# Chunked attention and a gated feed-forward in one kernel: transposes and value products on TensorE in 64x64 tiles instead of whole-array matmuls and transposing transfers

## Chip, cores and metric

One core of a Trainium2 chip. The metric is the device time of one execution in microseconds (us). Engines: TensorE (PE in the profile, its weight loads PEld), VectorE (DVE), ScalarE (ACT), GpSimd (POOL), SyncE (SP). Each executes its own instructions in the order in which they were recorded.

## What is computed

Four batches of 768 tokens, 8 heads of 64. Attention goes by chunks of 32 tokens: a chunk sees 8 memory rows, 16 tokens to the left, itself, and 8 tokens to the right, 64 keys in all.

```
for c in range(S // 32):
    k_full = concat(mem_k, k[c*32-16 : c*32+40])          # cut at the ends of the sequence
    a = softmax((q[c*32 : c*32+32] @ k_full.T) / 8)
    out[c*32 : c*32+32] = a @ concat(mem_v, v[c*32-16 : c*32+40])
x = out as [3072 tokens, 512]                              # heads side by side
result = (relu(x @ w_gate) * (x @ w_val)) @ w_out          # 512 -> 1536 -> 512
```

## The kernel before, in words

**Tiles and blocks.** The 3072 tokens are 24 tiles of 128 (six per batch, four chunks each). Tiles are gathered into blocks, `BLOCKS = [2, 2, 4, 4, 4, 4, 4]`, on which the feed-forward (FFN) works: `first` (L396) makes 12 x 2 groups of four matmuls (gate and value, 256 or 512 tokens wide), ScalarE's `relu` (L402) and VectorE's `gate` (L408) join them, `second` (L421) multiplies with w_out, `store` copies and sends the rows out on SP's queue.

**Attention of one tile.** q and k must stand with the head dimension on the partitions, so they are transposed. In batch 0 `pair_t` (L225) does it in 64-column tiles from pairs of tokens; for tiles 6 to 11 `qk_t` (L264) does it in whole-array transposes; from tile 12 on (`LATE_QK`) `qk_transfer` (L272) does it by a transposing transfer on SP's queue, and keys are copied from there to their place in `kT`. Then: `scores` (L298, 32 matmuls in 64x32 tiles of the array, two PSUM banks), `row_max`, `subtract` (VectorE), `exponent` (L326, three ScalarE instructions, which also bring the keys into the order of `v_bd`), `row_sum`, `reciprocal`, `normalise` (VectorE), the transpose of P (`p_t`, L347, whole-array; from tile 18 on `p_transfer`, L351, on SP's queue), `values`, and `x_copy` into the block's `xT`.

**Values.** For batches 1 to 3 two heads share a 128-row block of `v_bd`, `[128, 4, 24, 128]`, with zeros where a head's rows meet the other head's columns; L377 multiplies it in 16 whole-array matmuls of 32 columns. There are two such buffers: POOL zeroes each (L129, four memsets), POOL's queue loads the value rows over the zeros (L173), and eight transfers per batch (L156) put the memory rows in, from `vmem`. In batch 0 v comes as it lies, is brought to its chunks by `shift` (L204, products with a band matrix), and L363 and L370 multiply memory and value rows.

**PSUM.** Three pools: `fps`, four banks, FFN and shifts; `sps`, two banks, scores; `aps`, two banks, transposes and value products.

**What sets the order.** A planner in the kernel (`schedule`) walks through assumed durations, landing times and free buffers, takes for each engine the ready operation with the least priority value (attention ahead of FFN), and records the instructions in that order. So the order is fixed when the kernel is built, and at run time an engine waits for its next instruction whatever stands behind it. Loads are a list of their own on POOL's queue, with at most eight in flight. A transposing transfer is assumed to land 6 us after its issue (`LAND`); attention of a tile is held back until the FFN has come to a given group (`pace`).

Of the kernel before, what the change touches and what calls it, by code (L numbers as in the profile page):

```python
# [19 lines left out]
def kernel(  # L20
# [20 lines left out]
    CH = 32  # L41
# [7 lines left out]
    CTX = 16 + CH + 8  # L49
    NSET = 2  # L50
    BLOCKS = [2, 2, 4, 4, 4, 4, 4]
    GROUPS = [(0, 2), (2, 6), (6, 9), (9, 12)]
    BAND0 = 48

    LATE_QK, LATE_P = 12, 18

    KEY_RUNS = ((0, CH, 0), (KW, 64, CH), (CH, KW, CTX))
# [3 lines left out]
    ldpool = ctx.enter_context(tc.tile_pool(name="ldpool", bufs=18))  # L61
# [4 lines left out]
    ktpool = ctx.enter_context(tc.tile_pool(name="ktpool", bufs=3))  # L66
    grpool = ctx.enter_context(tc.tile_pool(name="grpool", bufs=3))
    opool = ctx.enter_context(tc.tile_pool(name="opool", bufs=3))

    fps = ctx.enter_context(tc.tile_pool(name="fps", bufs=4, space=bass.MemoryType.PSUM))  # L70
    sps = ctx.enter_context(tc.tile_pool(name="sps", bufs=1, space=bass.MemoryType.PSUM))
    aps = ctx.enter_context(tc.tile_pool(name="aps", bufs=2, space=bass.MemoryType.PSUM))
# [3 lines left out]
    def copy(eng, o, i):  # L76
# [5 lines left out]

    band = const.tile([128, BAND0 + 176], F16, name="band")
    ident_h = band[:, BAND0:BAND0 + 128]
    ident_b = const.tile([128, 128], BF16, name="ident_b")
    ident_f = const.tile([128, 128], F32, name="ident_f")
    w_gate_sb = const.tile([128, NFC, DFF], F16, name="w_gate_sb")
# [4 lines left out]
    vmem = const.tile([128, B, H, D], F16, name="vmem")  # L92
    vmem_0 = const.tile([128, HP, 2 * D], F16, name="vmem_0")
    v_bd = [const.tile([128, HP, NCH, 2 * D], F16, name=f"v_bd_{s}") for s in range(NSET)]
    vmem_f = v_bd[1][:, HP - 1].rearrange("p c d -> p (c d)").bitcast(F32)[:, 0:HP * 2 * D].rearrange(
        "p (h d) -> p h d", h=HP)
    v_q = v_bd[0][:, 0:2].rearrange("p h c d -> p (h c d)").rearrange("p (h c d) -> p h c d", h=HP, d=D)
    v_n = {}
    qk_p = {(i, r): const.tile([128, H, 2 * D], BF16, name=f"qk_p_{i}_{r}") for i in range(2) for r in range(TPB // 2)}
# [4 lines left out]
    def load_gate_val(i, which, par):  # L104

        m0, m1 = GROUPS[i]
        n = 128 * (m1 - m0)
        src, dst = ((moe_w_gate, w_gate_sb), (moe_w_val, w_val_sb))[which]
        nc.gpsimd.dma_start(
            dst[D * par:D * par + D, :, 128 * m0:128 * m1],  # L110
            bass.AP(tensor=src.tensor, offset=src[HP * D * par, 128 * m0].offset,
                    ap=[[DFF, D], [D * DFF, NFC], [1, n]]),
        )

    def make_band():
        nc.gpsimd.memset(band, 0.0)
        nc.gpsimd.affine_select(
            out=band, in_=band, compare_op=ALU.not_equal, fill=1.0, base=BAND0,
            pattern=[[-1, BAND0 + 176]], channel_multiplier=1)

    def load_out(i):
        n = NDC // 2
        nc.gpsimd.dma_start(
            w_out_sb[:, n * i:n * i + n, :],
            moe_w_out.rearrange("(c p) f -> p c f", p=128)[:, n * i:n * i + n, :],
        )

    def zero(eng, t, hp):
        eng.memset(t[:, hp].rearrange("p c d -> p (c d)").bitcast(F32), 0.0)  # L129


    def mem_load():
        for par in range(2):
            nc.sync.dma_start(
                kmem_f[:, par, :],
                bass.AP(tensor=mem_k.tensor, offset=mem_k[0, par, 0, 0].offset,
                        ap=[[2 * NMEM * D, B * HP], [D, NMEM], [1, D]]),
            )

    def mem_keys_t():  # L140
        TMP["kmem"] = aps.tile([128, B * HP * NMEM], F32, tag="aps", name="kmem_ps")
        nc.tensor.transpose(TMP["kmem"], kmem_f.rearrange("p a d -> p (a d)"), ident_f)

    def mem_values(par):
        p = 64 * par + CTX
        nc.gpsimd.dma_start(
            vmem[p:p + NMEM].rearrange("p b h d -> p (b h) d"),
            bass.AP(tensor=mem_v.tensor, offset=mem_v[0, 0, 0, 0].offset,
                    ap=[[D, NMEM], [NMEM * D, B * H], [1, D]]),
        )  # L150

    def mem_rows(eng, b, n):
        hp, par = divmod(n, 2)
        p = slice(64 * par + CTX, 64 * par + CTX + NMEM)
        src = vmem[p, b, HP * par + hp]
        eng.dma_start(  # L156
            v_bd[b % NSET][p, hp, :, D * par:D * par + D],
            bass.AP(tensor=src.tensor, offset=src.offset,
                    ap=[src.ap[0], [0, NCH], [1, D]]))


    def pattern_load():
        for par in range(2):
            p = 64 * par + CTX
            nc.sync.dma_start(
                vmem_f[p:p + NMEM, :, D * par:D * par + D],
                bass.AP(tensor=mem_v.tensor, offset=mem_v[0, HP * par, 0, 0].offset,
                        ap=[[D, NMEM], [NMEM * D, HP], [1, D]]))

    def load_v_rows(b, par, s0, s1, c0, c1):  # L170

        dst = v_bd[b % NSET].rearrange("p h c d -> p (h c) d")
        nc.gpsimd.dma_start(  # L173
            dst[64 * par + s0:64 * par + s1, c0:c1, D * par:D * par + D],
            bass.AP(tensor=v.tensor, offset=v[b, HP * par, 0, 0].offset + (CH * c0 + s0 - 16) * D,
                    ap=[[D, s1 - s0], [CH * D, c1 - c0], [1, D]]))

    def v_parts(b, par, c0, c1):
        parts = []
        if (b, par, c1) == (B - 1, 1, HP * NCH):  # L180
            c1 -= 1
            parts.append((b, par, 0, 48, c1, c1 + 1))
        return parts + [(b, par, 0, CTX, c0, c1)]


    def load_v_tile(t):
        v_n[t] = ldpool.tile([128, H, D], F16, tag="qk_b", name="v_n")
        nc.gpsimd.dma_start(
            v_n[t],
# [3 lines left out]
    def shift(c0):  # L193
        ps = TMP["sh", c0] = fps.tile([128, 2, HP, D], F32, tag="fps", name="vs_ps")
        for i in range(2):
            t, g = divmod(c0 + i, 4)
            parts = [(t, BAND0 + CH * g - 16)]
            if g == 0 and t:
                parts.append((t - 1, BAND0 + 112))
            if g == 3 and t < TPB - 1:  # L200
                parts.append((t + 1, BAND0 - 48))
            for n, (src, x) in enumerate(parts):
                for par in range(2):
                    nc.tensor.matmul(ps[D * par:D * par + D, i], lhsT=band[:, x:x + 64],  # L204
                                     rhs=v_n[src][:, HP * par:HP * par + HP, :],
                                     start=(n == 0), stop=(n == len(parts) - 1))

    def shift_copy(c0, eng):
        copy(eng, v_q[:, :, c0:c0 + 2, :].rearrange("p h c d -> p c h d"), TMP.pop(("sh", c0)))


    qk_b, qT, kT = {}, {}, {}

    def load_pair(r, i):
        x = (q, k)[i]
        nc.gpsimd.dma_start(
            qk_p[i, r],
            bass.AP(tensor=x.tensor, offset=x[0, 0, 256 * r, 0].offset,
                    ap=[[2 * D, 128], [S * D, H], [1, 2 * D]]))

    def pair_t(r, i, j):
        ps = TMP["pair", r, i, j] = aps.tile([128, HP, 128], BF16, tag="aps", name="qk_ps")
        for h in range(H):
            p = D * (h % 2)
            nc.tensor.transpose(ps[p:p + D, h // 2, :], qk_p[i, r][:, h, D * j:D * j + D], ident_b)  # L225

    def pair_copy(r, i, j, eng):
        ps = TMP.pop(("pair", r, i, j))
        if i == 0:
            o = qT[0][:, :, 256 * r + j:256 * r + 256]  # L230
            copy(eng, bass.AP(tensor=o.tensor, offset=o.offset, ap=[o.ap[0], [S, HP], [2, 128]]), ps)
        else:
            o = kT[0][:, :, 8 * r:8 * r + 8, j:KW]
            copy(eng,
                 bass.AP(tensor=o.tensor, offset=o.offset,
                         ap=[o.ap[0], [NCH * KW, HP], [KW, 8], [16 + NMEM, 2], [2, 8]]),
                 ps.rearrange("p h (c x s) -> p h c x s", c=8, x=2))

    def load_qk(a, i):
        b, t = divmod(a, TPB)  # L240
        x = (q, k)[i]
        qk_b[a, i] = ldpool.tile([128, H, D], BF16, tag="qk_b", name="qk_b")
        nc.gpsimd.dma_start(  # L243
            qk_b[a, i],
            bass.AP(tensor=x.tensor, offset=x[b, 0, 128 * t, 0].offset,
                    ap=[[D, 128], [S * D, H], [1, D]]))
# [11 lines left out]
    P_n, PT, S_ps, SM, TMP = {}, {}, {}, {}, {}  # L258

    def qk_t(a, i):  # L260
        ps = TMP["qk", a, i] = aps.tile([128, HP, 128], BF16, tag="aps", name="qk_ps")
        x = qk_b.pop((a, i))
        for hp in range(HP):
            nc.tensor.transpose(ps[:, hp, :], x[:, 2 * hp:2 * hp + 2, :].rearrange("p h d -> p (h d)"), ident_b)  # L264

    def qk_transfer(a, i):
        b, t = divmod(a, TPB)
        if i == 0:
            o = qT[b][:, :, 128 * t:128 * t + 128]
        else:  # L270
            o = TMP["qk", a, i] = ktpool.tile([128, HP, 128], BF16, name="k_t")
        nc.sync.dma_start(o, qk_b.pop((a, i)).rearrange("p h d -> p (h d)"), transpose=True)  # L272

    def qk_copy(a, i, eng):
# [505 lines left out]
```

## Time and profile before

| | |
|---|---|
| median of 3 runs | 252.5 us (252.33 to 255.31) |
| profiled execution, its own time | 254.24 us |
| its span, first to last instruction | 252.5 us |
| mean granted TensorE clock | 0.986 |
| busy: PE, DVE, ACT, POOL | 234.0, 131.3, 115.0, 90.7 us |
| software queue (POOL's): packets, MB | 94368, 16.42 |
| hardware queue (SP's): packets, MB | 21888, 10.51 |

The page's slices are a fortieth of the span each, 6.3 us. A group's row has its line, engine, operation, tiles, shape and count, then busy us and the mean ns of one. A timeline row has start and length in us, and in brackets the idle time of the engine before it and what ended it. The length of a matmul row holds the time in which its results drain while the next one runs already, so what a matmul costs its successor is read from start to start.

### The profile page before, as it was taken

The page shows a single profiled execution, that of the slowest core. Times are in us where ns is not written, and L with a number is a line of the kernel's source. Part 1 is how long each engine was busy: PE and PEld are TensorE (multiplying, and loading weights), DVE is VectorE, ACT ScalarE, POOL GpSimd, SP SyncE. Part 2 cuts the span into 40 slices and gives each one's busy share as a digit, 9 for nine tenths or more (in the row PEclk, how much of TensorE's full clock was granted, in tenths as well). Part 3 has the DMA queues.
Part 4 walks back from the last instruction along what each step waited for, and adds up shares of the span by engine and source line. Part 5 has one row for each costly group of instructions (what it writes and reads, how often), then busy time and mean ns, then how long its engine had stood idle before and what let it go on. Part 6 is the DMA issues. An engine that isn't in the chain of part 4 may idle for free.

```text
span 252.5 us, 6081 instructions
## 1 busy us (share of the span) xinstructions
PE 234.0 (93%) x2529; PEld 128.7 (51%) x2529; DVE 131.3 (52%) x245; ACT 115.0 (46%) x250; POOL 90.7 (36%) x105
## 2 busy tenths in 40 slices
PE   1869999999899999799999949999999999999994
PEld 0647887884445555345444424455444544444443
DVE  2462657985158886588543817964049340133400
ACT  2856757763236555356334444543153531333212
POOL 8975899605179950298450060000000000000000
PEclk9999999999999999999999976999999999999999
DMA  7999999999999999999999999222221101300022
GB/s 79 174 179 203 201 84 130 204 156 97 176 203 139 140 135 86 123 211 136 123 116 123 122 138 169 42 44 41 86 83 23 21 0 54 116 1 0 0 85 84
DMA packets 116285, 27.32 MB, mean 108 GB/s; under 512 B 107297, under 2 KB 113185, under 8 KB 116257
## 3 DMA queue, kind: packets, MB, share of 16 engines
q0 software_dynamic: 94368, 16.42, 113.4%
q1 hardware_dynamic: 21888, 10.51, 24.3%
q8 instruction: 20, 0.33, 0.6%
q14 instruction: 9, 0.07, 0.1%
HBM read 32.06 MB, written 6.29 MB: 152 GB/s over the span
## 4 chain that ended last, share of the span: by engine, by line
PE 79%; DMA 12%; DVE 4%; ACT 3%; issue 1%; POOL 0%; SPq 0%; ACTq 0%; POOLq 0%
PE v_ps L396 25%; PE g_ps L396 25%; PE out_ps L421 18%; DMA k_t<-qk_b 9%; PE s_ps L298 2%; PE xT_ps L377 2%; DMA qk_p<-in_q_dram 2%; PE xT_ps L370 2%; PE vs_ps L204 1%; PE qk_ps L225 1%; PE pT_ps L347 1%; DVE mx L311 1%; DVE dif L318 1%; PE qk_ps L264 1%; PE xT_ps L363 1%
## 5 line engine op out<-in xcount | busy, mean ns | idle before, releaser
L408 DVE TENSOR_TENSOR gvT<-v_ps,g_relu 128x512 f16<-128x512 f32 (+1 forms) x84 | 51.3, 611 | 51.9 <-PE v_ps L396 48.9
L396 PE MATMUL g_ps<-xT,w_gate_sb 128*128 128x512 f16 (+1 forms) x336 | 77.4, 353 | 0.8 <-ACT xT L78 0.8
L396 PE MATMUL v_ps<-xT,w_val_sb 128*128 128x512 f16 (+1 forms) x336 | 77.8, 355 | 0.0
L402 ACT ACTIVATE g_relu<-g_ps 128x512 f16<-128x512 f32 (+1 forms) x84 | 45.0, 535 | 56.2 <-PE g_ps L396 55.9
L421 PE MATMUL out_ps<-w_out_sb,gvT 128*128 128x512 f16 (+2 forms) x300 | 64.9, 371 | 0.0
L396 PEld LDWEIGHTS <-w_gate_sb 128*128 128x128 f16 x336 | 31.7, 99 | 28.3 <-issue 2.0
L396 PEld LDWEIGHTS <-w_val_sb 128*128 128x128 f16 x336 | 31.7, 99 | 27.2 <-issue 1.5
L421 PEld LDWEIGHTS <-gvT 128*128 128x128 f16 x300 | 28.2, 98 | 31.3
L78 ACT COPY o_sb<-out_ps 128x512 f32<-128x512 f32 (+2 forms) x25 | 14.1, 565 | 36.4 <-PE out_ps L421 32.5
L311 DVE TENSOR_REDUCE mx<-s_ps 128x8 f32<-128x512 f32 x24 | 16.4, 683 | 18.7 <-PE s_ps L298 18.2
L326 ACT ACTIVATE p_exp<-dif 128x256 f16<-128x256 f32 (+2 forms) x72 | 19.6, 336 | 10.7 <-DVE dif L318 10.5
L243 POOL DMA_DIRECT2D qk_b<-in_k_dram x18 | 16.4, 911 | 14.4 <-issue 8.0
L330 DVE TENSOR_REDUCE sm<-p_exp 128x8 f32<-128x512 f16 x24 | 16.3, 681 | 9.2 <-ACT p_exp L326 9.0
L156 POOL DMA_DIRECT2D v_bd<-vmem x16 | 10.1, 637 | 28.6 <-DMA v_bd<-in_v_dram 27.4
L243 POOL DMA_DIRECT2D qk_b<-in_q_dram x18 | 16.4, 909 | 3.8 <-issue 2.5
L341 DVE TENSOR_TENSOR p_n<-p_exp,rinv 128x512 f16<-128x512 f16 x24 | 16.5, 687 | 0.4
L318 DVE TENSOR_TENSOR dif<-s_ps,mx 128x512 f32<-128x512 f32 x24 | 16.5, 686 | 0.4
L173 POOL DMA_DIRECT2D v_bd<-in_v_dram x7 | 13.9, 1996 | 5.2 <-issue 3.7
L298 PE MATMUL s_ps<-kT,qT 64*32 64x64 bf16 (+2 forms) x768 | 8.6, 199 | 5.7 <-ACT kT L78 3.3
L298 PEld LDWEIGHTS <-qT 64*32 64x32 bf16 x768 | 5.3, 92 | 14.0 <-issue 11.8
L78 ACT CAST xT<-xT_ps 128x512 f16<-128x512 f32 x14 | 8.2, 586 | 8.5 <-PE xT_ps L377 4.5
L377 PEld LDWEIGHTS <-v_bd 128*128 128x128 f16 x288 | 9.4, 97 | 3.6 <-issue 0.3
(52 smaller groups left out, 159.8 us busy)
## 6 DMA issues: line engine op xcount, KB each, us to landing
out_dram<-o_sb SPq DMA_DIRECT2D x23, 256.0 KB
v_bd<-in_v_dram POOLq DMA_DIRECT2D x5, 672.0 KB, 18.0
qk_b<-in_k_dram POOLq DMA_DIRECT2D x18, 128.0 KB, 7.5
qk_b<-in_q_dram POOLq DMA_DIRECT2D x18, 128.0 KB, 7.8
w_out_sb<-in_moe_w_out_dram POOLq DMA_DIRECT2D x2, 768.0 KB, 11.6
qk_p<-in_k_dram POOLq DMA_DIRECT2D x3, 256.0 KB, 6.1
qk_p<-in_q_dram POOLq DMA_DIRECT2D x3, 256.0 KB, 6.5
v_n<-in_v_dram POOLq DMA_DIRECT2D x6, 128.0 KB, 6.5
```

The source lines that it names most:

```text
L78: nc.scalar.copy(o, i)
L243: nc.gpsimd.dma_start(qk_b[a, i], bass.AP(tensor=x.tensor, offset=x[b, 0, 128 * t, 0].offset, ap=[[D, 128], [S * D, H], [1, D]]))
L298: nc.tensor.matmul(s[CH * g:CH * g + CH, r, o0:o0 + hi - lo], lhsT=qT[b][d, h2, CH * c:CH * c + CH], rhs=keys[d, h2, lo:hi], start=True, s ...
L311: nc.vector.reduce_max(SM[a, "mx"], s4, axis=AX.X)
L318: nc.vector.tensor_tensor(out=SM[a, "dif"].rearrange("p (m r) a s -> p r m a s", r=2), in0=S_ps.pop(a).rearrange("p r (m a) s -> p r m a s ...
L326: nc.scalar.activation(p[:, :, :, s0:s0 + k1 - k0], dif[:, :, :, k0:k1], ACT.Exp, scale=SCALE)
L330: nc.vector.reduce_sum(SM[a, "sm"], SM[a, "p"], axis=AX.X)
L341: nc.vector.tensor_tensor(out=P_n[a], in0=SM.pop((a, "p")), in1=rinv_b, op=ALU.mult)
L396: nc.tensor.matmul(ps, lhsT=w[:, f, 128 * m:128 * m + 128], rhs=xTs[blk][:, f, :], start=(f == 0), stop=(f == NFC - 1))
L402: nc.scalar.activation(st["r", m], st.pop((0, m)), ACT.Relu)
L408: nc.vector.tensor_tensor(out=st["gv"][:, m, :], in0=st.pop((1, m)), in1=st.pop(("r", m)), op=ALU.mult)
L421: nc.tensor.matmul(st["o", t, c], lhsT=st["gv"][:, m, 128 * t:128 * t + 128], rhs=w_out_sb[:, m, c[0]:c[1]], start=(m == 0), stop=(m == ND ...
```

## The change

- PSUM is one tile of eight banks, and the planner hands out banks by number (`bank_of`); at most 6 are with attention (4 for tiles past the first batch) and 5 with the FFN.
- q and k of all batches come as in batch 0, as pairs of tokens (pieces of 256 bytes in place of 128). Their transposes, and those of P, are matmuls on four 64x64 tiles of the array: rows in two halves `r`, results on two halves of the partitions; the two halves `r` go to two banks. `qk_t`, `qk_transfer` and `p_transfer` are gone.
- v is `v_sb[b]`, `[128, 4, 24, 64]`, one buffer per batch, without zero blocks: rows 0 to 63 are heads 0 to 3, rows 64 to 127 heads 4 to 7. A POOL copy (`mem_rows`) spreads the memory rows over the whole buffer, then four transfers write the 32 rows before and the 24 behind them. Value products are 32 matmuls of 64x64 tiles.
- Keys keep one order, so `exponent` is one instruction.
- `BLOCKS = [2, 2, 2, 4, 4, 4, 4, 2]`; w_gate and w_val come in one transfer per group instead of two; the band matrix is replaced by `sel`.
- Attention is held back by time: a tile of a block from the third on may begin when the FFN reaches the operation that stands `LEAD - STEP * j` = 33 - 5.2 j us of assumed FFN time ahead of the block's begin.

```
-    LATE_QK, LATE_P = 12, 18
-    KEY_RUNS = ((0, CH, 0), (KW, 64, CH), (CH, KW, CTX))
+    psum = pspool.tile([128, 8, 512], F32, name="ps")
+    def banks(key, dt=F32):
+        b0, b1 = bank_of[key]
+        x = psum[:, b0:b1 + 1:b1 - b0]
+        return x.bitcast(dt) if dt != F32 else x
...
+    def mem_rows(eng, b):
+        src = vmem[:, H * b:H * b + HP, :]
+        copy(eng, v_sb[b],
+             bass.AP(tensor=src.tensor, offset=src.offset, ap=[src.ap[0], [D, HP], [0, NCH], [1, D]]))
...
+    def pair_t(n, i):
+        ps = banks(("t", n, i), BF16)[:, :, 0:512].rearrange("p r (j h s) -> p r j h s", j=2, h=HP)
+        x = qk_p.pop((n, i))
+        for j in range(2):
+            for h in range(H):
+                p = D * (h % 2)
+                for r in range(2):
+                    m = slice(64 * r, 64 * r + 64)
+                    nc.tensor.transpose(ps[p:p + D, r, j, h // 2, :], x[m, h, D * j:D * j + D], ident_b[m, m])
...
     def p_t(a):
-        for hp in range(HP):
-            nc.tensor.transpose(ps[:, hp, :], x[:, hp].rearrange("p a s -> p (a s)"), ident_h)
+        for hp in range(HP):
+            for par in range(2):
+                for r in range(2):
+                    m = slice(64 * r, 64 * r + 64)
+                    nc.tensor.transpose(ps[64 * par:64 * par + 64, r, hp, :], x[m, hp, par, :], ident_h[m, m])
...
     def values(a):
+        four = [(r, c) for c in range(2) for r in range(2)]
+        if b == 0:
+            for n in range(2):
+                for r, c in four:
+                    m = slice(64 * r, 64 * r + 64)
+                    nc.tensor.matmul(ps[64 * c:64 * c + 64, r, n, :], lhsT=vmem_0[m, 2 * n + c, :],
+                                     rhs=x[m, 2 * n + c, :], start=(n == 0), stop=False, skip_group_check=True)
-        for hp in range(HP):
-            for g in range(4):
-                r = slice(CH * g, CH * g + CH)
-                nc.tensor.matmul(ps[:, hp, r], lhsT=v_bd[b % NSET][:, hp, 4 * t + g, :],
-                                 rhs=x[:, hp, r], start=True, stop=True)
+        for n in range(2):
+            for g in range(4):
+                w = slice(CH * g, CH * g + CH)
+                for r, c in four:
+                    m = slice(64 * r, 64 * r + 64)
...
+                        nc.tensor.matmul(ps[64 * c:64 * c + 64, r, n, w], lhsT=v_sb[b][m, 2 * n + c, 4 * t + g, :],
+                                         rhs=x[m, 2 * n + c, w], start=True, stop=True)
...
+    def load_v_op(b):
+        load(("mr", b), 0, 6.5, lambda: mem_rows(nc.gpsimd, b), [("vm", 0), ("vm", 1)])
+        for r in range(2):
+            for i, (s0, s1) in enumerate(((0, M0), (M0 + NMEM, 64))):
...
     for b in range(1, B):
+        n = TPB // 2 * b
+        load_pair_op(n, 1)
+        load_pair_op(n, 0)
+        load_pair_op(n + 1, 1)
+        load_v_op(b)
+        load_pair_op(n + 1, 0)
+        load_pair_op(n + 2, 1)
+        load_pair_op(n + 2, 0)
```

## The prediction

> **What bounds the kernel now.** I read the page first (busy shares, slices, granted clock), then the table of stretches, the chain that ended last, and then TensorE's own timeline, from which every price below is taken.
>
> ```profile
> PE 234.0 (93%) x2529; PEld 128.7 (51%) x2529; DVE 131.3 (52%) x245; ACT 115.0 (46%) x250; POOL 90.7 (36%) x105
> ...
> PE   1869999999899999799999949999999999999994
> ...
> PEclk9999999999999999999999976999999999999999
> ```
> TensorE (PE) is the bound in nearly every slice; VectorE and ScalarE are half idle. There are dips near 104 and 148 us, and the clock falls behind the second. The stretches around that one (length, busy us and count of PE, PEld, DVE, ACT, POOL, clock, DMA share, GB/s) say how much:
>
> ```profile
> 140.00:150.00 10.00, 6.65 (x112) 3.50 (x111) 4.70 (x10) 2.92 (x8) 3.95 (x5) 0.93 1.89 133
> 150.00:160.00 10.00, 10.00 (x111) 4.07 (x111) 8.25 (x16) 5.92 (x16) 0.00 (x0) 0.73 1.19 126
> ```
> The chain of waits names what PE waited for there (start, length): keys transposed by a transfer.
>
> ```profile
> 95.44 11.57 DMA k_t<-qk_b
> ...
> 136.70 12.23 DMA k_t<-qk_b
> ```
> PE's timeline (start, length, ..., idle before) has the two waits, and the price of each kind of matmul, if starts are subtracted: the length of a row holds the drain that the next row overlaps.
>
> ```profile
> 37.68 0.60 PE L396 MATMUL v_ps<-xT,w_val_sb 128*128 128x256 f16 x4
> 38.21 0.64 PE L225 MATMUL qk_ps<-ident_b,qk_p 128*64 128x128 bf16 x16
> 38.78 0.61 PE L396 MATMUL g_ps<-xT,w_gate_sb 128*128 128x256 f16 x4
> ```
> ```profile
> 90.51 1.03 PE L396 MATMUL g_ps<-xT,w_gate_sb 128*128 128x512 f16 x4
> 91.47 0.31 PE L298 MATMUL s_ps<-kT,qT 64*32 64x64 bf16 x32
> 91.71 0.40 PE L347 MATMUL pT_ps<-band,p_n 128*128 128x128 f16 x4
> 91.94 1.03 PE L396 MATMUL v_ps<-xT,w_val_sb 128*128 128x512 f16 x4
> 92.80 1.03 PE L396 MATMUL g_ps<-xT,w_gate_sb 128*128 128x512 f16 x4
> 93.67 0.55 PE L377 MATMUL xT_ps<-pT,v_bd 128*128 128x32 f16 x16
> 94.07 1.02 PE L396 MATMUL v_ps<-xT,w_val_sb 128*128 128x512 f16 x4
> ```
> ```profile
> 107.39 0.29 PE L298 MATMUL s_ps<-kT,qT 64*32 64x64 bf16 x26 [1.54 <-DVE kT L80]
> ...
> 149.62 0.39 PE L298 MATMUL s_ps<-kT,qT 64*32 64x64 bf16 x26 [3.35 <-ACT kT L78]
> 149.94 1.89 PE L396 MATMUL v_ps<-xT,w_val_sb 128*128 128x512 f16 x4
> 151.63 1.91 PE L396 MATMUL g_ps<-xT,w_gate_sb 128*128 128x512 f16 x4
> ```
> What to see: four gate matmuls take 0.86 (91.94 to 92.80), but 0.96 when scores follow (90.51 to 91.47), and 0.53 ahead of L225 (37.68 to 38.21) against 0.44 ahead of another group (33.03 to 33.47): going from whole-array matmuls into tiles costs about 0.09. The way back shows in the single rows: the last score starts 0.12 before the next weight load. A tile's own steps, from the same single rows, are 28 ns for the scores (8 tiles at once, 3.5 ns from matmul to matmul), 31.5 for L370 (64 weight columns, 32 moving), 56 for L225 (128 moving). Whole-array transposes take 0.23 per four (91.71 to 91.94), L377 0.40 per tile of tokens with no switch.
>
> **The change part by part.**
>
> *PE work, moved and added.* I count from the first gate matmul on, in the order in which the changed kernel's instructions stand. A 64x64 step with 64 moving columns lies between L370's 31.5 ns and L225's 56; as the scores do 64 columns in 28, I take 36 (nearer L370, same weight columns), ends 31.5 and 50.
> - Pure matmul time. Before: 704 scores x 3.6 ns = 2.5, 46 shifts x 56 = 2.6, 24 L225 x 28 = 0.7, 64 P transposes and 48 L264 and 16 memory products x 56 = 7.1, 128 L370 x 15.8 = 2.0, 288 L377 x 25 = 7.2: 22.1 us. After, four tiles at once: 672 scores 2.4, 34 shifts 1.9, 608 q/k transposes x 36/4 = 5.5, 352 P transposes 3.2, 32 memory products x 56/4 = 0.45, 704 value products x 31.5/4 = 5.5: 18.9 us. So -3.2, though 12 q, 12 k and 6 P transposes come back from the transfers.
> - Switches. Before: 27 entries, 28 exits, 4 changes between tilings: 27 x 0.09 + 32 x 0.115 = 6.1 us, since L264, L347 and L377 are whole-array and switch nothing. After, all of them are tiles: 71 entries, 72 exits, 11 changes: 6.4 + 9.5 = 15.9. So +9.8.
> - Two blocks of two tiles for one of four: 192 matmuls of 216 ns become 384 of 109: +0.25.
> Sum +6.85 us, all on the path. With 31.5 ns it is +5.6, with 50 +9.9; if a switch costs nothing in the new mode, -3.0.
>
> [...]
>
> *Waits removed.* Nothing waits for a transposing transfer any more: 1.54 at 107.39, 0.65 at 110.7 (the next score's idle 0.49 and what trails it), 3.35 at 149.62, and the half clock behind that: three groups of 1.7 instead of 0.86 and a slow value product, 2.6. The page's 0.8 before the first gate matmul at 69.40 goes too: it waited for ScalarE's copy of tiles 6 and 7, and the third block is now tiles 4 and 5, whose values are there 15 us of PE work ahead. Sum -9.0. What is late next? In the new order each later tile has some 6 us of PE work between score and P transpose, for a chain of about 3.6 (four DVE steps of 0.69, one of 0.19, one ACT step of about 0.6), 1.9 from there to its values, and from the fifth block on x is complete 9 to 20 us early. I see nothing that takes their place. Lower bound: the profiled execution took 254.24 (span 252.47 and 1.77 around it), the median of the three runs is 252.5; if those 1.7 are such waits, only 7.3 are to be had.
>
> *Start.* PE runs at half rate until 25.7 by the trace's clock records (four P transposes last 0.61 at 15.31, 0.39 at 30.12). Rows on the path to the first x: q's 16 transposes and two ScalarE copies, 7.63 to 9.63, become 32 quarter matmuls and one copy each on two engines (about -0.7); exponent 0.81 to 0.6; memory and value products 0.52 + 0.97 to about 0.9, per tile. VectorE gets copies in between and takes some back, and 12 more shifts and half a pair's transposes now stand before the first gate matmul. I take -1.0, ends 0 and -2.5.
>
> *One new wait.* The values of tile 2 stand right behind its P transpose, with ScalarE's 0.59 copy between them: +0.7 (0.5 to 0.8).
>
> *Transfers and POOL.* POOL loses eight memsets (10.7 us) and 16 issues of memory rows; SP's queue loses 30 transposes and 8 issues and keeps the stores. q/k come in 256-byte pieces, 18 issues for 36. New: three POOL copies of 6144 elements ahead of each batch's values. Nearest rows: memset 1536 elements in 1.40 (0.9 ns each, so 5.6 us), affine select 224 f16 elements in 0.37 (1.65 ns, 10.1 us); I take 7.5, since the select's row holds a fixed part. Queued behind it are the four value transfers of batch 1 and all later q/k. The last start-up load lands at 35.0 as before; then vmem 1.5, w_out 5.5 (between the landings at 44.55 and 58.51, less one value transfer), three pairs 4.3: queue empty at 46.4. The copy ends at 36.5 + 7.5 = 44, the first value transfer is issued by 45.3, and 17 us (two of 8.5 between the landings at 58.51 and 67.01) make 63.4. PE asks for tile 6's values after 41.9 us of work: 21.2 + 1.7 (half clock) + 41.9 + 0.7 = 65.5. So hidden, with 2 us to spare; cost 0, upper end in the second rival.
>
> *ScalarE, VectorE, PSUM.* One exponent for three (0.81 to 0.6, x24), k copies in two halves, q copies back for 12 tiles: hidden under PE, VectorE at 52%. A bank comes back 1.6 us or more of PE work after its last writer, in all but a few places, so the FFN is not starved: 0, at most +0.3.
>
> Sum: +6.85 - 9.0 - 1.0 + 0.7 = -2.45. The profiled execution would take 251.8; the median, 252.5 now, **250.1 us**.
>
> **Rivals.**
> 1. Switches overlap: the new mode's weights are loaded while the FFN runs, so half of the 15.9 us goes: 242. For it: L377's small products pay nothing. Against: every tiling in this trace pays 0.09 and 0.115, the 64-column one of L370 too. With only entries free (6.4): 243.7; with a quarter free, 246.
> 2. Slower: tile 6's values are late. POOL's copy is 4 to 5 us longer than my upper end, or batch 1's transfers slower. It decides from a landing at 69: then PE stands still 3.4 us, and as behind 149.62 the clock halves for another 2.6, so 250.1 + 6 = 256. For it: only 2 us of slack, and a copy that no row shows. Against: POOL's rows per element, and a queue with less in it.
> 3. The four tiles do not run four at once: tiles of the same rows alternate. The steps of q/k, P and values double: +14.6 and some 2 at the start, 267. This is the change not doing what it says. Against it: the scores' 3.5 ns.
> 4. The clock falls to half in a stretch of tile work. [...] Here the clock stayed at half through 7.6 busy us between 10 and 20, until gate matmuls ran, and later fell only in the 3.35 us without a matmul; the longest stretch without FFN in the new order is 1.9 us. If it fell once, +2.6: 252.7, inside my band.
>
> **How the numbers follow.** Forecast (small gain, within 2%) 0.55, rival 1 0.17, rival 2 0.14, rival 3 0.06, rival 4 0.03, others 0.05 split over both sides. The likeliest case's own range is 247 to 254, from the step of 31.5 to 50 ns and the start. For 8 in 10 I reach to a quarter of the switches free and a somewhat better start (245.5) and to the late values (257). Measurements of this kernel tell about 2%, or 5 us, from no change (three runs span 3 us). Faster by more than that (under 247.4) 0.24: most of rival 1 and the forecast's edge; slower (over 257.5) 0.18: rival 3, rival 2 where the wait is longer, half of the others; 0.58 between.
>
> **What would show it.** No idle over 1 us before a score; granted clock 1.00 from the first gate matmul on; 0.53 before each burst where 0.44 is pure, and 0.12 behind; 32 q/k transposes in about 0.40, start to next start; values about 0.37 against L377's 0.40; first gate matmul near 21; POOL's copy 5.6 to 10 us; tile 6's values waiting for nothing. I am wrong if bursts cost nothing to enter, if PE's attention work falls below 35 us after the first gate matmul, or if PE idles for over 2 us before tile 6's values.

## The result, and the profile after

| | before | after |
|---|---|---|
| median of 4 runs each on one chip | 253.13 us | 280.46 us (280.18 to 281.65) |
| profiled execution, its own time | 254.24 us | 280.22 us |
| its span | 252.5 us | 278.4 us |

The changed kernel is slower: ratio 1.107, 95% interval 1.099 to 1.116. The forecast was 250.1 us (245.5 to 257.0), so it missed by 30 us and on the wrong side. (A kernel at times runs some per cent slower here, e4 below in 306.78 and in 317.56 us; where that happened, the ratio is that of the undisturbed runs alone, while medians and spreads are of all.)

The page of the kernel after: busy time, slices, granted clock, the chain that ended last, and the rows of the FFN's matmuls (busy us and mean ns, then the idle time ahead of them). In this kernel L223 transposes q and k, L264 makes the scores, L319 transposes P, L346 makes the value products, L364 and L385 are the FFN's two steps, and L71 and L73 copy on ScalarE and VectorE.

```profile
PE 238.7 (86%) x3873; PEld 130.9 (47%) x3873; DVE 147.9 (53%) x292; ACT 113.8 (41%) x222; POOL 69.9 (25%) x67
...
PE   1646699988978999769999799999899978899995
...
PEclk9975999999999999999999999999999999999999
...
PE 79%; DVE 10%; issue 4%; ACT 4%; DMA 2%; POOL 0%; DVEq 0%; ACTq 0%; POOLq 0%
...
L364 PE MATMUL ps<-xT,w_gate_sb 128*128 128x256 f16 (+1 forms) x384 | 78.7, 328 | 8.8 <-DVE mx L279 2.8
L364 PE MATMUL ps<-xT,w_val_sb 128*128 128x256 f16 (+1 forms) x384 | 78.3, 327 | 3.6 <-ACT pT L71 1.4
...
L385 PE MATMUL ps<-w_out_sb,gvT 128*128 128x512 f16 (+2 forms) x300 | 66.3, 371 | 2.6 <-issue 1.4
```
TensorE is busy 4.7 us longer, but 86% of the span for 93%: it waits. The two dips of the kernel before are gone; many small ones, all over the kernel, have come. Most of them lie ahead of the FFN's own matmuls (L364, 12.4 us; L385, 2.6), of which the first step in the kernel before waited only 0.8 us, once. The releaser is odd: a gate matmul reads weights and x and writes its own bank, and row max (L279) reads scores. The waits of all engines (us in total, times, longest) show it both ways:

```profile
DVE dif L286 <- PE ps L364: 6.0, 6, 1.4
...
PE ps L364 <- DVE xT L73: 3.4, 4, 0.9
...
PE ps L364 <- DVE mx L279: 2.8, 4, 1.0
...
PE ps L364 <- DVE dif L286: 2.1, 3, 0.9
```
If the return of a score's banks were late, it would be the subtract (L286) that releases them, since it reads the scores last; row max never gives a bank back. The rows of the subtract and of the copy of x (L73) alone would leave a late return open. But the subtract waits for FFN matmuls (first row), of which it reads nothing. The timeline of all engines has one full turn of this:

```profile
238.25 0.43 PE L346 MATMUL ps<-pT,v_sb 64*64 64x32 f16 x32
...
238.62 1.04 PE L364 MATMUL ps<-xT,w_val_sb 128*128 128x512 f16 x4
...
239.76 0.69 DVE L73 CAST xT<-ps 128x512 f16<-128x512 f32 x1 [1.50 <-PE ps L364]
...
240.50 1.02 PE L364 MATMUL ps<-xT,w_gate_sb 128*128 128x512 f16 x4 [0.85 <-DVE xT L73]
```
The values of tile 23 are done at 238.7. By the planner's list they stand in banks 0 and 7, the value matmul at 238.62 writes bank 5, the gate matmul at 240.50 bank 1. The copy of x, a view of banks 0 and 7, waits until bank 5 is written; then the gate matmul into bank 1 waits until the copy ends. They have no bank in common; banks 1 and 5 lie between 0 and 7. These waits are in the program: its list of waits has 136 between instructions without a common bank. Whether they come from what lies between the two banks of a view is what the first experiments try.

The prices of the forecast, in TensorE's timeline (start to start):

```profile
76.05 0.69 PE L346 MATMUL ps<-pT,v_sb 64*64 64x32 f16 x64
76.67 0.61 PE L364 MATMUL ps<-xT,w_gate_sb 128*128 128x256 f16 x4
...
79.48 0.60 PE L364 MATMUL ps<-xT,w_val_sb 128*128 128x256 f16 x4
80.01 0.45 PE L223 MATMUL ps<-ident_b,qk_p 64*64 64x64 bf16 x32
80.39 0.28 PE L364 MATMUL ps<-xT,w_gate_sb 128*128 128x256 f16 x1
...
89.61 0.32 PE L319 MATMUL ps<-ident_h,p_n 64*64 64x64 f16 x16
89.86 0.39 PE L364 MATMUL ps<-xT,w_val_sb 128*128 128x256 f16 x2
```
32 q/k transposes take 0.38, 16 of P 0.25, 64 value products (two tiles of tokens) 0.62, and a group ahead of a burst 0.53. These prices came out as forecast; the time is in the waits.

### The profile page after: what moved, and what is told of

Its sections match the earlier page's. It is cut to its first block, busy times and chain, and to the rows that moved or that the text cites. A ratio compares the mean times of both kernels' runs of the same rounds, so it can differ in the third digit from the quotient of the medians.

```text
span 278.4 us, 8694 instructions
## 1 busy us (share of the span) xinstructions
PE 238.7 (86%) x3873; PEld 130.9 (47%) x3873; DVE 147.9 (53%) x292; ACT 113.8 (41%) x222; POOL 69.9 (25%) x67
## 4 chain that ended last, share of the span: by engine, by line
PE 79%; DVE 10%; issue 4%; ACT 4%; DMA 2%; POOL 0%; DVEq 0%; ACTq 0%; POOLq 0%
PE ps L364 44%; PE ps L385 23%; PE ps L223 3%; DVE mx L279 2%; PE ps L264 2%; DVE dif L286 2%; PE ps L346 2%; DMA qk_p<-in_q_dram 2%; PE ps L319 2%; PE ps L195 2%; DVE gvT L376 1%; ACT pT L71 1%; DVE xT L73 1%; ACT g_relu L370 1%; ACT xT L71 1%
## 5 line engine op out<-in xcount | busy, mean ns | idle before, releaser
L364 PE MATMUL ps<-xT,w_gate_sb 128*128 128x256 f16 (+1 forms) x384 | 78.7, 328 | 8.8 <-DVE mx L279 2.8
L364 PE MATMUL ps<-xT,w_val_sb 128*128 128x256 f16 (+1 forms) x384 | 78.3, 327 | 3.6 <-ACT pT L71 1.4
L376 DVE TENSOR_TENSOR gvT<-ps,g_relu 128x256 f16<-128x256 f32 (+1 forms) x96 | 52.8, 552 | 38.9 <-PE ps L364 18.9
L370 ACT ACTIVATE g_relu<-ps 128x256 f16<-128x256 f32 (+1 forms) x96 | 46.9, 490 | 61.7 <-PE ps L364 58.9
L385 PE MATMUL ps<-w_out_sb,gvT 128*128 128x512 f16 (+2 forms) x300 | 66.3, 371 | 2.6 <-issue 1.4
L364 PEld LDWEIGHTS <-w_gate_sb 128*128 128x128 f16 x384 | 36.1, 98 | 35.3 <-issue 8.9
L364 PEld LDWEIGHTS <-w_val_sb 128*128 128x128 f16 x384 | 34.4, 98 | 23.5 <-issue 4.5
L385 PEld LDWEIGHTS <-gvT 128*128 128x128 f16 x300 | 27.5, 98 | 33.3 <-issue 3.7
L71 ACT COPY o_sb<-ps 128x512 f32<-128x512 f32 (+2 forms) x25 | 14.2, 568 | 40.3 <-PE ps L385 40.0
L73 DVE COPY qT<-ps 128x512 bf16<-128x512 bf16 x12 | 8.7, 729 | 32.0 <-PE ps L223 31.8
L279 DVE TENSOR_REDUCE mx<-ps 128x8 f32<-128x512 f32 x24 | 16.6, 690 | 13.6 <-PE ps L264 6.9
L286 DVE TENSOR_TENSOR dif<-ps,mx 128x512 f32<-128x512 f32 x24 | 16.5, 687 | 9.0 <-PE ps L364 6.0
L292 ACT ACTIVATE p_exp<-dif 128x512 f16<-128x512 f32 x24 | 15.1, 630 | 13.3 <-DVE dif L286 13.2
L169 POOL DMA_DIRECT2D v_sb<-in_v_dram x13 | 16.6, 1283 | 1.2 <-POOL v_sb L73 1.2
L307 DVE TENSOR_TENSOR p_n<-p_exp,rinv 128x512 f16<-128x512 f16 x24 | 16.4, 685 | 0.3
L73 POOL COPY v_sb<-vmem 128x6144 f16<-128x6144 f16 x3 | 15.9, 5313 | 1.4 <-DMA vmem<-in_mem_v_dram 1.4
L223 PE MATMUL ps<-ident_b,qk_p 64*64 64x64 bf16 x768 | 12.1, 204 | 4.8 <-DMA qk_p<-in_k_dram 1.5
L223 PEld LDWEIGHTS <-qk_p 64*64 64x64 bf16 x768 | 9.3, 117 | 12.1 <-issue 8.7
L71 ACT COPY pT<-ps 128x512 f16<-128x512 f16 x14 | 8.2, 586 | 14.2 <-DVE dif L286 5.5
L71 ACT CAST xT<-ps 128x512 f16<-128x512 f32 x15 | 8.8, 585 | 11.8 <-PE ps L346 7.1
```

The costliest lines, as they stand in the source:

```text
L71: nc.scalar.copy(o, i)
L73: eng.tensor_copy(o, i)
L169: nc.gpsimd.dma_start(dst[64 * r + s0:64 * r + s1, c0:c1, :], bass.AP(tensor=v.tensor, offset=v[b, HP * r, 0, 0].offset + (CH * c0 + tok) * D,
L223: nc.tensor.transpose(ps[p:p + D, r, j, h // 2, :], x[m, h, D * j:D * j + D], ident_b[m, m])
L279: nc.vector.reduce_max(SM[a, "mx"], s4, axis=AX.X)
L286: nc.vector.tensor_tensor(out=SM[a, "dif"].rearrange("p (m r) a s -> p r m a s", r=2), in0=score_view(a).rearrange("p r (m a) s -> p r m a ...
```

## The experiments

**Which coupling?** Four kernels, three theories (stated in the first expectation). e1 hands out only neighbouring banks as pairs:

```
-                            bank_of[key] = sorted(free_banks[:o["ps"]])
...
+        pairs = [[b, b + 1] for b in free if b + 1 in free]      # pick(2, free_banks)
```


> Three theories. Enclosed banks: a view of two banks that do not lie side by side (banks 1 and 5, say) is ordered as if it held the banks between them too, so a gate matmul in bank 3 waits for the row max that reads banks 1 and 5, and the other way round; the changed kernel's list of waits holds 136 between instructions that have no bank in common. Shared banks: the FFN really gets banks whose last reader is late. Short assumed times: the planner's 0.16 to 0.45 us per burst of tiles lack the 0.2 us of going in and out, so its hand-over of banks is early. This kernel hands out only neighbouring banks for pairs, everything else alike (the order on TensorE nearly line for line); no enclosing view is left. Enclosed banks: the 17 us of idle time ahead of L364 mostly go, no L364 waits for mx any more, 250 to 262 us. Shared banks and short times: both are as before, 274 us or more.

Measured: 263.55 us, just past the range; ratio to before 1.047 (1.045 to 1.050). Every engine has the same instructions in the same order as in the kernel after. Of the idle time ahead of L364 and L385, 15.0 us in the kernel after (the expectation's 17 was too many), 2.1 are left, none put down to VectorE:

```profile
PE ps L364 <- issue: 1.8, 1, 1.8
...
PE ps L385 <- issue: 0.3, 1, 0.3
```

e2 and e3 give FFN and attention four banks each, with the same plan in both:

```
+    PAIRS, OWN = [(0, 1), (2, 3)], [4, 5, 6, 7]      # e2
+    PAIRS, OWN = [(0, 4), (2, 6)], [1, 3, 5, 7]      # e3
```


> The FFN and the shifts own four neighbouring banks, attention the other four in two fixed neighbouring pairs, as before the change. No bank is shared between FFN and attention, and no view encloses a bank of another. Enclosed banks and shared banks both say that the idle time ahead of L364 goes: 250 to 264 us (attention has four banks for six at the start, which may cost 1 to 3). Short assumed times: 272 or more.

> The same plan as the run with own banks, instruction for instruction, with the banks only renumbered: attention's pairs are 0 and 4, 2 and 6, the FFN's banks 1, 3, 5, 7. Nothing is shared, but every pair encloses two of the FFN's banks; the list of waits holds 190 between instructions without a common bank. Enclosed banks: as slow as the changed kernel or slower, 275 to 300 us. Shared banks, and short assumed times: the same time as the run with own banks, within 1 us.

Measured: e2 262.47 us, 1.043 (1.038 to 1.047); e3 300.96 us, 1.195 (1.192 to 1.198). The groups of e2, then of e3:

```profile
L364 PE MATMUL ps<-xT,w_gate_sb 128*128 128x256 f16 (+1 forms) x384 | 79.1, 329 | 1.8 <-issue 1.8
L364 PE MATMUL ps<-xT,w_val_sb 128*128 128x256 f16 (+1 forms) x384 | 78.9, 329 | 0.0
```
```profile
L364 PE MATMUL ps<-xT,w_gate_sb 128*128 128x256 f16 (+1 forms) x384 | 80.1, 333 | 8.1 <-DVE dif L286 4.6 <-DVE xT L73 1.3 <-ACT xT L71 1.1
L364 PE MATMUL ps<-xT,w_val_sb 128*128 128x256 f16 (+1 forms) x384 | 79.8, 332 | 6.0 <-DVE dif L286 1.6 <-DVE pT L73 1.4 <-ACT pT L71 1.3
```
The same instructions in the same order, no bank shared between FFN and attention in either: numbers alone cost 38 us (some 5 of it by a consequence that is shown below: two normalises of 2.51 and 3.53 us beside POOL's copies, for 0.69). So it is the enclosed banks, and sharing costs little or nothing (e1 shares, and its ratio is within 0.5% of e2's).

e4 corrects the planner's assumed times (`{"PE": 0.28}` to `0.48` for q/k and so on).

> The changed kernel with the planner's assumed TensorE times set to what its own trace shows from start to start, entry included: q/k transposes 0.48 for 0.28, scores 0.35 for 0.26, P 0.35 for 0.16, shifts 0.50 for 0.40, values 0.46 for 0.32 (batch 0: 0.58 for 0.45). Nothing else is edited; banks are still any free ones (182 waits between instructions without a common bank). Short assumed times: 255 to 264 us. Enclosed banks: still 272 or more. Shared banks: part of it goes, 265 to 275.

Measured: 312.38 us (306.78 to 318.31), 1.219 (1.217 to 1.222). Short assumed times are not the cause; with more waits between instructions that share no bank (182 for 136) it got slower still (the order of the instructions changed as well).

**What is left in e1?** Waits that the page calls "issue", inside bursts. TensorE's timeline of e1:

```profile
18.84 0.36 PE L264 MATMUL ps<-kT,qT 64*32 64x64 bf16 x24
22.56 0.25 PE L264 MATMUL ps<-kT,qT 64*32 64x64 bf16 x8 [3.35 <-issue]
...
54.12 0.37 PE L223 MATMUL ps<-ident_b,qk_p 64*64 64x64 bf16 x21
57.49 0.37 PE L223 MATMUL ps<-ident_b,qk_p 64*64 64x64 bf16 x11 [2.99 <-issue]
```
TensorE stops in the middle of 32 scores and of 32 transposes. The instruction queue's row of the pages (packets, MB), before and e1:

```profile
q8 instruction: 20, 0.33, 0.6%
```
```profile
q8 instruction: 30, 0.49, 0.8%
```
A packet is 16384 bytes in the traces, and the kernels have 5058 and 7746 matmuls and weight loads: 253 and 258 to a packet, some 64 bytes for each (estimates from these counts). The waits of e1 stand multiples of 256 instructions apart, within one. From its trace, every multiple with a wait over 0.6 us:

```
TensorE passes    packet runs       next multiple runs    wait
 446th  16.89     20.18 - 21.07      702nd  22.56         3.35
1214th  34.69     38.34 - 39.28     1470th  40.61         0.85
1726th  51.13     54.52 - 56.05     1982nd  57.49         2.99
2494th  74.54     77.36 - 78.25     2748th  79.63         1.82
```
In these four, with the DMA engines eight or nine tenths busy (e1's slices to 105 us), the packet starts 2.8 to 3.7 us after TensorE has passed the multiple before, and TensorE goes on 1.3 to 1.5 us after the packet's end. From the first column to the fourth, 256 instructions took 5.1 to 6.4 us. In e1 the clock fell behind two of these waits; three stretches of it (length, busy us and count of PE, PEld, DVE, ACT, POOL, clock, DMA share, GB/s):

```profile
57.00:60.40 3.40, 2.91 (x23) 1.89 (x22) 1.21 (x3) 1.13 (x3) 3.15 (x1) 0.50 1.90 173
60.40:80.90 20.50, 18.40 (x402) 10.24 (x402) 11.45 (x24) 9.04 (x18) 12.54 (x11) 1.00 1.98 192
80.90:84.30 3.40, 3.40 (x49) 2.15 (x47) 3.07 (x6) 1.18 (x3) 3.40 (x1) 0.50 1.82 183
```
Behind the waits of 2.99 and 1.82 it is at half for 3.4 us each: seven groups of the FFN take 0.66 to 0.99 for 0.44 to 0.53, and a burst of scores 0.35 for 0.24, 2.8 us in all. Not every long wait does it: in e9 below, one of 3.25 us at 54.92 left the clock whole. The times at which the granted clock changed in e1 (26.26, 56.98, 60.39, 80.87, 84.29) lie whole multiples of 3.41 us apart. In the 3.41 us ahead of its falls e1 had 2.48 and 1.82 us of waiting; e9's wait, with such steps counted on from the rise of its clock at 25.84, is split into 1.64 and 1.61. That is a reading of these traces and was not tested.

e7 adds 64 tiny matmuls ahead of the first transposes.

> The run with neighbouring banks and 64 tiny matmuls more (8 columns, tiles of 64x64, result not used; 128 instructions) ahead of the transpose of the memory keys, where TensorE waits for q and k anyway until 6.1 us. Instruction blocks: the waits without a semaphore stay at the 702nd, 1470th, 1982nd or 2748th instruction, give or take a few, counted with the new ones, so they move 128 instructions forward in the work: no longer ahead of the scores of tile 2, for instance. Time 257 to 267. Rival (they belong to the work): they stay ahead of the same instructions, so at the 830th and 2109th, and the time is 263 to 265.

Measured: 263.37 us (one run). The waits over 0.6 us stand at the 447th (0.72), 957th (1.39), 2237th (1.53), 3003rd (2.53) and 3515th (1.97) instruction, all 702 + 256 n within three, though at other multiples than the four named, and in front of other work: the scores of tile 2 run through. The places belong to the count, not to the work.

e9 reads q, k and v of batches 1 to 3 in long pieces (`ap=[[H * 2 * D, 128], [1, H * 2 * D]]`), so their elements stand in other places.

> The run with neighbouring banks, but q, k and v of batches 1 to 3 are read in long pieces (2 KB for 256 bytes, 12 KB for 128): as many bytes to the same tiles, with the elements in other places, so the attention of these batches is computed on permuted input. Everything else is alike, every instruction of TensorE too. Instruction blocks: in the run with neighbouring banks each packet of the instruction queue began 2.9 to 3.9 us after TensorE had passed a multiple of 256 instructions while the loads ran, and 0 us after they had ended at 105 us. With the DMA engines free earlier the packets come at once from some 50 us on, the waits at the 1982nd, 2748th and 3515th instruction (2.99, 1.82, 0.33) go, the ones at the 702nd and 1469th stay: 257 to 260 us. Rival (the waits belong to the work): 262 to 264, or less only as far as a load was waited for.

Measured: 262.27 us, 1.040 (1.032 to 1.047). The wait at the 3515th went, 2747th fell to 1.38, 1981st stayed (3.25), and a new one of 1.33 came at the 2237th: a miss, with a time in the rival's range. The loads only moved forward: the slices show the DMA engines nine tenths busy to 71 us all the same. It told nothing apart. e15 and e16 do, with 256 tiny matmuls at 84 or at 215 us.

```
+        for i in range(256 if (blk, m, which) == (2, 4, 0) else 0):      # e16: (6, 4, 0)
+            nc.tensor.matmul(ps[64 * c:64 * c + 64, 0:8], lhsT=ident_b[0:64, 0:64], rhs=ident_b[0:64, 0:8], ...)
```


> The run with neighbouring banks (263.6) and 256 tiny matmuls more (64x64 tiles, 8 columns, result not used; 512 instructions) ahead of the gate matmuls of block 2, column group 4, at some 84 us, while the loads run. The work itself is 2 to 4 us (8 to 16 ns each). Instruction blocks: two multiples of 256 more fall into those 2 us, and while the loads run a block came 5.2 to 6.4 us after the one before it had been passed, so TensorE is held for 8 to 10 us more: 271 to 278 us. Rival (no such limit): 265 to 268.

> The same 256 matmuls ahead of the same group of block 6, at some 215 us, when the loads have long ended. Instruction blocks: a packet began 0 us after the multiple was passed there, lasted about 1.0 and TensorE went on 1.4 after its end, so two blocks in a row take some 5 us, of which the work hides 2 to 4: 266 to 270 us, and 4 us or more below the run with the same work at 84 us. Rival: the same time as that run within 1 us.

Measured: 276.23 us, 1.097 (1.089 to 1.104), and 270.42 us, 1.075 (1.070 to 1.081). TensorE in e15, then in e16:

```profile
82.83 1.21 PE L365 MATMUL ps<-ident_b 64*64 64x8 bf16 x40
86.30 3.58 PE L365 MATMUL ps<-ident_b 64*64 64x8 bf16 x128 [2.26 <-issue]
92.22 1.23 PE L365 MATMUL ps<-ident_b 64*64 64x8 bf16 x40 [2.34 <-issue]
```
```profile
216.36 4.72 PE L365 MATMUL ps<-ident_b 64*64 64x8 bf16 x254
221.91 0.21 PE L365 MATMUL ps<-ident_b 64*64 64x8 bf16 x2 [0.83 <-issue]
```
Between the two waits of e15 lie exactly 128 matmuls with their 128 weight loads (the view's window cuts the first row; 88 ran ahead of the first wait). The same work costs 5.8 us more in the time of the loads: waits of 4.6 for 0.8, and a clock at half for 17.1 us (80.67 to 97.73) for 6.8. The work itself was dearer than I had put it (19 ns a matmul, not 8 to 16), so e16 lies just past its range. In e16 the clock fell at 219.63 behind no wait: in the 3.3 us before, TensorE ran 205 of the tiny matmuls without a pause.

**Parts undone.** e5 and e6, on e1: P, then q and k of batches 1 to 3, by the whole array again (`nc.tensor.transpose(ps[:, hp, :], ..., ident_h)`, one bank).

> Starts from the run with neighbouring banks (263.6 us). What is left there beside the forecast are waits of TensorE that no semaphore explains: 3.35 us ahead of its 702nd instruction, 0.85 ahead of the 1469th, 2.99 ahead of the 1981st, 1.82 ahead of the 2747th, 0.33 ahead of the 3515th, together 9.3 us, all a multiple of 256 instructions apart, all while the loads run. Theory of instruction blocks: instructions come 256 at a time over the DMA engines (the page: 30 packets of 0.49 MB on the instruction queue, 20 of 0.33 MB before), bursts of tiles use them up faster than they come while the loads fill the engines. Rival: these waits belong to the work in front of which they stand (late q and k, late x). Here P alone is transposed by the whole array again (4 matmuls for 16, one bank for two, no way into tiles and back): 24 x 0.2 = 4.9 us of switches less, 576 of 7746 instructions less, so 2 blocks less. Blocks and the forecast's switch price: 254 to 260 us. If switches cost nothing: 262 to 264.

> As the last one, and q and k of batches 1 to 3 too are transposed by the whole array, tokens as they lie (8 matmuls for 32 per pair of tiles; the loads go back to 128-byte pieces, two for one; the key copies are one instruction for two). Batch 0 stays as it is. 864 instructions less again, about 25 blocks for 30; 18 x (0.38 + 0.2 - 0.46) = 2.2 us of TensorE less. Blocks and switch price: 248 to 257 us, and the waits without a semaphore fall below 6 us in sum. Rival (the waits belong to the work): they stay at 9 us or grow, since the loads have more pieces: 257 to 262.

Measured: e5 262.13 us, 1.046 (1.032 to 1.060), a miss and inside the rival's range; e6 262.0 us, spread over 255 to 267, 1.024 (0.984 to 1.063), with a median past its range. In e5 I had priced a switch at 0.2 beside the 0.25 of the burst, which holds the way out already: only 24 x 0.09 and 24 x 0.02 were to be had, 2.7 us. TensorE's busy time is 2.3 lower (236.1 for 238.4). But a wait of 2.13 is new: VectorE's copy of the memory keys (L244), 0.31 to 0.68 in e1, lasted 5.50 beside a POOL copy, and a gate and TensorE behind it. In e6 one issue wait is left (2.24), as expected, but here too POOL's copy got in the way, with a wait of 3.85:

```profile
64.02 5.32 POOL L73 COPY v_sb<-vmem 128x6144 f16<-128x6144 f16 x1
...
64.55 5.36 DVE L333 TENSOR_TENSOR p_n<-p_exp,rinv 128x512 f16<-128x512 f16 x1
...
69.96 0.61 PE L342 MATMUL ps<-ident_h,p_n 128*128 128x128 f16 x4 [3.85 <-DVE p_n L333]
```
The normalise lasts 5.36 for 0.69, until POOL's copy has ended. e10 cuts the copy in four (`for h in range(HP): copy(eng, v_sb[b][:, h], ...)`).

> The run with P and q/k on the whole array, with POOL's copy of the memory rows in four pieces (one per head pair, 1536 elements each, about 1.3 us) for one of 5.33 us. In that run a normalise on VectorE that began at 64.55, 0.5 us after such a copy, lasted 5.36 us for 0.69, until the copy's end, and TensorE stood still for 3.84 behind it; row max, subtract and gate ran beside such copies at their usual length. Theory: an instruction of VectorE with both inputs in SBUF waits for POOL's copy to end. Then no normalise lasts over 2.1 us, the wait of 3.84 goes, and the clock that fell behind it too: 251 to 257. Rival (VectorE waited for something else there): the normalise is as long as before, 256 to 262.

Measured: 258.99 us (256.26 to 266.89), 1.023 (1.017 to 1.029). The expectation was wrong on the remedy:

```profile
63.94 5.69 POOL L73 COPY v_sb<-vmem 128x1536 f16<-128x1536 f16 x4
...
65.09 5.09 DVE L334 TENSOR_TENSOR p_n<-p_exp,rinv 128x512 f16<-128x512 f16 x1
...
70.24 0.40 PE L343 MATMUL ps<-ident_h,p_n 128*128 128x128 f16 x4 [3.59 <-DVE p_n L334]
```
The normalise ends only behind the last piece, at 70.18 for 69.63. e13 has ScalarE copy the rows, e14 adds the blocks of before; e11 and e12 are the same two with own banks and POOL's pieces.

> The run with P and q/k of batches 1 to 3 on the whole array and neighbouring banks, with the memory rows copied by ScalarE in eight pieces of 768 elements per batch, so that POOL copies nothing. VectorE's normalise was held for 5.4 and 5.1 us by POOL's copy in one piece and in four, with 3.84 and 3.58 us of idle TensorE behind it; that goes, and part of the clock lost behind it. Against 256.2 of span: 250 to 254 of span, 250 to 256 us, about as the kernel before. Rival: ScalarE's 16 us of copies delay relus and so the FFN: 255 to 262.

> As the last, with the blocks of before (2, 2, 4, 4, 4, 4, 4): 0.2 to 1 us less by the forecast's price, or up to 2 more if x of the third block is late.

> Own banks for the FFN (262.5 us alone), P and q/k of batches 1 to 3 on the whole array, POOL's copies in four pieces: what stays of the change are values and scores in tiles, batch 0 in tiles, v without zero blocks and no transfers. By the parts: about as the run with POOL's pieces, 250 to 257; rival: four banks for attention instead of six bring waits of their own, 256 to 262.

> As the last, with the blocks of before (2, 2, 4, 4, 4, 4, 4). By the forecast's price of two blocks of two tiles for one of four (0.25 us and two ways into tiles less): 0.2 to 1 us less than the last. Rival: x of the third block is complete later, as at 69.40 in the kernel before, and the time is up to 2 us more.

Measured: e13 255.81 us, 1.017 (1.013 to 1.022), and no normalise over 0.9 us; e14 257.7, 1.024 (1.020 to 1.029), so the blocks of before are not better there; e11 263.11 us (258.94 to 268.49), 1.030 (1.024 to 1.036), in the rival's range, but its trace has two normalises of 7.08 and 6.67 us that ended behind POOL's pieces, so four banks are not shown to be the reason; e12 between 251.9 and 266.7, no comparison. e13 is the best form of the change that I found, and it does not beat the kernel before.

e8 is the kernel before with one part of the change alone (`LATE_QK, LATE_P = 24, 24`).

> The kernel before with one part of the change alone: no transposing transfers, q, k and P of all tiles transposed by the whole array. By the forecast's own terms: waits -9.0, 24 x 0.23 = 5.5 for q and k and 6 x 0.23 = 1.4 for P come back to TensorE, sum -2.1: 247 to 252 us. Rival: the waits turn into others (the two banks of the attention pool now serve 30 transposes more): 252 to 260.

Measured: 253.42 us, 1.011 (0.994 to 1.028): past its range, and no difference shown. The waits for transfers are gone from its trace, and the clock does not fall between 25.13 and 250.41 us. TensorE's busy time rose by 2.7 us (236.7 for 234.0), and waits of 2.1 and 1.1 ahead of P's transposes stand where 1.4 stood.

## Why the prediction was wrong

- **PE work +6.85: right in its prices.** q/k 0.38 (0.40 forecast), P 0.25 (0.25), values 0.37 and 0.31 per tile (0.37), a way into tiles 0.09. Two of its bounds do not follow from its counts: steps of 31.5 and 50 ns give +5.8 and +10.2, not +5.6 and +9.9, and free switches in the new mode alone some -9, not -3.0; the outcome does not hang on them. Rival 3 was off: 32 q/k transposes took 0.38 from start to start, where its doubled steps make some 0.7 (an estimate from the forecast's own 0.29 of steps and 0.115 of way out). The ways into tiles are paid (0.53 for 0.44, as forecast), so rival 1 was off.
- **The step that failed**: "A bank comes back 1.6 us or more of PE work after its last writer, in all but a few places, so the FFN is not starved: 0, at most +0.3", and with it "I see nothing that takes their place". I asked when each bank comes back, and e1 shows that this answer was right. What I did not ask is what a pair view of banks b0 and b1 is ordered against. The built program's list of waits answers it: 136 waits between instructions without a common bank, 41 of them on TensorE, 60 on VectorE, 35 on ScalarE; none in e1 and e2, 190 in e3. The old pools kept FFN and attention apart in PSUM; the one tile with pairs like 0 and 7 ties nearly all of them together, in both directions. Cost: 280.46 to 263.55, 17 us (15 by the ratios).
- **The term that was missing.** Instructions were priced by their matmul time alone; 7746 for 5058 is in the forecast nowhere. In e1 the late blocks cost 9.3 us, in the kernel after 6.8, since other waits hide some.
- **Start -1.0: wrong by that term.** First gate matmul at 25.93, not 21.2; in e1 at 24.88, of which 3.35 is the wait at the 702nd instruction: 21.5.
- **Waits removed -9.0: they went, the gain did not show.** e8 takes them away alone and is not faster, against -2.1 expected; its interval reaches to a gain of 1.6 at most.
- **New wait +0.7: right** (0.70 at 29.85 in e1; 1.56 in the kernel after, where ScalarE's copy waited for a subtract). **POOL's copies: hidden, as forecast**; 5.31 each was less than the 7.5 taken and than its lower bound of 5.6. Tile 6's values wait for nothing, so rival 2 was off. **Clock**: in the kernel after it does not fall from 27.1 us to the end of the work; in e1 it does, for 2.8 us in all, but behind waits and not in tile work, so rival 4 was off here. In e16 it fell in tile work, after 3.3 us of tiny matmuls without a pause; the forecast's longest stretch without FFN was 1.9.

The sum: 251.8 for the profiled execution, + 16.4 of enclosed banks (280.2 to e1's 263.8), + 9.3 of late instructions, + 2.8 of clock behind them = 280.3, for 280.2 measured. That e1's waits can be set against the forecast like this takes its other terms as right; only the parts above were tried alone, the waits removed did not show their full gain, and that the sum closes to 0.1 us is luck.

## What to carry to other kernels

When PSUM is one tile whose banks are handed out by number, let every access hold neighbouring banks (17 us here), and look for waits between instructions that share none: an engine that waits for a reader of data that it does not touch is the sign. Cutting matmuls into tiles multiplies instructions, so set their number per microsecond against the rate at which they came in here while the loads ran (256 in 5.1 to 6.4 us, in e1). A count of PE time can be right to 0.02 us per burst and the forecast still be 30 us off, if what the instructions wait for is not followed through the program.

## What the runs showed of the hardware that I had not expected

- TensorE's instructions came in packets of 16384 bytes, some 256 to a packet (30 packets for 7746). In the four blocks of e1 that TensorE waited for over 0.6 us, all before 80 us, with the loads running, a packet began 2.8 to 3.7 us after TensorE had passed the multiple before, and 256 instructions took 5.1 to 6.4 us. From 105 us on in e1, with the loads nearly over (the last ends at 111.8), it began 0.9 us after at most.
- VectorE's normalise, with both inputs in SBUF, lasted 5.36 us beside POOL's copy of SBUF (e6), and 5.09 beside four pieces of it (e10), for 0.69; in e5 a bf16 copy from SBUF to SBUF lasted 5.50, for 0.31 to 0.68. Each ended 0.2 to 0.6 us behind POOL's copy. Row max, row sum, subtract and gate beside such copies had their usual 0.69, 0.68, 0.69 and 0.42 (in the kernel after, 81.67 to 86.99). What sets the two kinds apart was not tried. In the kernel after no normalise and no copy of the memory keys fell beside a copy of POOL's.
